# Two-layer tail of an attention kernel on one core: the last plain 256 rows as a seven-product block multiplication, with the whole instruction order replaced

## The chip, the cores and the metric

The kernel runs on one core of a Trainium2 chip. A core has five engines with queues of their own: TensorE (PE, matmuls), VectorE (DVE), ScalarE (ACT), GpSimd (POOL) and SyncE (SP). They wait for each other by semaphores. GpSimd and SyncE are used here mainly to issue DMAs; GpSimd's run on one DMA queue (q0 in the profile), SyncE's on another (q1), and 16 DMA engines move the data of both. The metric is the device time of one execution in microseconds, as the median of several runs.

## The reference

```python
def _attn_ref(q, k, v):                      # q, k, v: (8, 12, 448, 64)
    S = q.shape[2]
    scale = 1.0 / np.sqrt(q.shape[-1])
    scores = scale * np.matmul(q, k.transpose(0, 1, 3, 2))
    attn = np.maximum(scores, 0.0) ** 2 / S
    return np.matmul(attn, v).astype(np.float32)

def _moe_ref(x, w_in, w_out):                # x: (3584, 768), w_in: (768, 2048), w_out: (2048, 768)
    h = x @ w_in
    g = 0.5 * h * (1.0 + erf(h / sqrt(2)))
    return (g @ w_out).astype(np.float32)
```

The output of the attention, with its 12 heads of 64 laid side by side, is the x of the two layers. There is no softmax: the scores are clipped at zero and squared.

## The kernel before

**Tiles.** The work goes by batch b (8 of them, 448 rows each) and, within the attention, by group g of four heads (3 of them). All matmuls take bf16. A score step (`fn_qk` in `add_steps`, matmuls at L744) is four matmuls of 64 x 64 tiles into a PSUM tile `ps`; ScalarE or VectorE clips it into `a_sq` (L756 or L758), VectorE squares it (L765). Seven score steps make a group, and `add_av` (L805) multiplies them with v into `pav`, which is copied into xT. The first layer of batches 0 to 3 is done in plain tiles (`add_f1`, six matmuls of 448 columns at L857, then Gelu on ScalarE); that of batches 4 to 7 by block products with seven multiplications (`add_block`, L1009).

**The second layer.** The rows of all batches, 3584, are cut into 14 groups of 256 (g = 0 to 13 in `add_group`). A group is a product of a 256 x 2048 by a 2048 x 768 matrix, cut into 2 x 2 blocks and done with seven block multiplications in place of eight. For that VectorE makes, once, four sums of w_out's quadrants (`add_tsums`, L1120, in two halves each; the third one overwrites a quadrant of w_out itself), and for each group four sums of h's blocks (`sum_op`, L1170). The seven products p1 to p7 (`product`, eight matmuls of 384 columns at L1191) go through two PSUM banks "f" at a time; evictions (`passed`, copies at L518 or L520, adds at L1225) pass the partial results on. Group 0, the first 256 rows of batch 0, is the exception before: it is done by `add_plain` as four tiles (two of rows by two of columns, 16 matmuls of 384 columns each, L1295), with one copy and, for each row tile, one store behind it.

**Turning q and k.** TensorE needs q and k with the head dimension on partitions. For batches 0 and 1 TensorE transposes them (L612, L640). From batch 2 on SyncE issues DMA transpositions (`turn` in `add_T_dma`, L667): per batch six, for each group one of q (into qT, from nq) and one of k (into kT, from nk). Half of each group's qT is then swapped between partition halves (`swapped`, by VectorE as two copies at L518 or by SyncE as two DMAs). The buffers nq and nk are single from batch 2 on, so the load of q of batch 3 (L464, by GpSimd) overwrites what the transposition of batch 2 has to have read.

**Loads.** GpSimd issues all loads in its queue: q (L464), k (L553), v (L571), w_in in five steps (L481 to L483), w_out in three steps of one, two and two DMAs (L487). At most eight of them are in flight: each waits for the semaphore of the eighth before it.

**The order.** No engine's order follows from the program's loops. The program adds 1471 operations with their dependencies to a list (`sch.add`), and the string `ORDER` says in which order they are issued: a letter for the engine (P TensorE, D VectorE, A ScalarE, G GpSimd, S SyncE) and the operation's number in the list; `Z1056` is a short filler matmul. The framework puts in the semaphore waits that the data need. Operations with a choice of engine (the clipping, copies, swaps) get it from the letter. Some numbers that matter below, the same in both kernels: S229 and S228 are the transpositions of q and k of batch 2, group 0, S232 and S231 of group 1, S235 and S234 of group 2; G238, G239 and G241 are the three steps of the w_out load, G149 the first part of v of batch 2, G270 the first load of q of batch 3. What `ORDER` takes from:

```python
    GROUPS = {2: (1,), 3: (2, 3), 4: (4, 5), 5: (6,)}
    ...
            flow += [(2.6, add_plain(t, n)) for n in (1, 0) for t in (0, 1)]
            add_tsums()
    ...
        flow += [y for g in GROUPS.get(b, ()) for y in add_group(g)]
```

Of the kernel before, what the change touches and what calls it, by code (L numbers as in the profile page):

```python
# [100 lines left out]
D287 P312 P300 A355 P318 S399 P362 D281 D313 D296 P364 A363 D319 P370 D278 A301 A365 P358 A371  # L101
P315 P306 A359 P282 P352 D307 P360 A353 G241 P376 A361 P368 A377 A283 P366 A369 D284 D302 D236
D293 P372 A367 D290 P374 A373 P378 D390 D316 G274 P327 A379 P297 D391 A328 G273 G155 P333 P339
D314 A334 G240 P382 D298 D305 D317 A340 A375 S398 D308 A299 D320 D329 P330 P324 D417 P309 A325
P380 A383 A331 D310 D311 D392 P342 P321 P336 A381 A337 D332 D418 D341 D419 D326 S402 P384 A322
S401 D393 P387 D396 A385 S405 D394 D400 G407 G242 G237 A323 A343 G409 S386 G275 S404 P443 P446
D335 D420 G408 A444 P421 D395 D344 A447 D338 P449 D388 A450 D397 S389 A422 G412 P452 P345 D445
D346 P437 G411 P423 A453 A438 P440 A347 D424 D403 P455 S542 A441 P425 A456 D439 D442 P473 A426
P470 P461 P427 D454 A471 A474 D462 P429 D428 D457 P464 P479 P476 D430 A480 P431 D448 A465 D451
G414 G415 P433 D472 A477 D432 D562 D406 P467 P458 A468 S435 D469 P485 P491 S545 A486 D434 P509  # L110
D459 A492 S541 P513 A510 D560 A460 D478 D561 P503 S544 A514 P494 P500 D563 P519 A501 D481 D463
P515 A520 D475 A504 A495 D493 P517 D466 D543 S547 D496 D487 P488 A518 P482 A516 D502 S548 G552
P497 P511 D498 S436 G555 D499 P523 G551 A512 D489 A483 G550 A484 G416 P525 A524 D490 D546 G554
P600 G413 P609 P606 G410 D610 P521 D505 A601 A607 P603 P506 D604 A526 A522 P612 P639 D507 P531
A640 P527 G558 D613 D605 A532 D508 G557 P618 A528 P624 P615 D619 P529 S705 S704 A616 P537 S708
A530 A625 P535 A538 D620 D549 D626 D602 P627 P636 A536 P657 A637 P533 D611 D614 S707 A628 D608
D629 P539 A534 A658 P564 A540 D641 D659 D617 D638 P566 A565 P630 S710 S711 P633 P621 D631 A634
D632 S709 G715 P642 P651 A622 D635 P568 G718 G714 A623 D567 A652 G717 P570 G559 A569 D643 D706
P648 P666 P663 A649 P572 G721 A667 G722 D571 D644 D664 P660 P654 P645 G719 D661 A655 G716 G553
G556 D662 D650 G720 P769 P763 P574 A764 D573 D665 D668 A646 P576 A770 A647 D575 D580 S578 P772  # L120
P775 P778 P584 D577 S836 A776 A779 D656 D581 D653 D765 P586 S835 A585 A773 D777 P787 P766 D582
P669 A767 D587 A788 D712 P781 P588 A670 A671 D768 D780 D774 A782 D789 P790 P796 A791 P590 D783
D583 A797 D771 P799 A589 P784 S839 S842 A800 D591 P802 D801 P793 P592 D803 D785 A794 S838 P594
D593 D786 P596 D595 D837 P805 P811 D597 P823 A806 S841 P674 D792 A824 D795 D723 D798 P672 S843
D812 A675 P678 S598 D804 D807 P814 P817 P808 A815 D818 A673 D724 A679 P874 P820 A809 P676 D821
G849 D813 D825 P682 A677 G846 A875 G844 G851 P684 G847 A683 D840 G850 G845 A810 P829 A685 P880
G713 P826 G852 A830 P680 D827 D828 P688 A681 A881 D831 D816 D822 D819 P686 A689 P889 A687 P877
P832 D890 A878 P886 P904 D833 A887 S947 P690 D834 G848 G853 D905 P892 A691 P883 P692 A893 D884
D888 P901 A693 P898 P910 A911 P698 S950 D906 D882 D899 D885 D894 D876 P696 A699 S946 P694 D725
A697 S599 A902 D879 D912 P702 A695 P700 A703 D903 D726 P727 A701 D900 D891 P916 S949 P907 P895  # L130
D917 A908 A728 S948 P928 P913 D929 D909 P731 A914 S953 A896 D915 D918 P729 A897 S951 D930 P925
P922 S952 P919 D926 A923 D730 S579 P931 D927 D732 P934 A920 P733 A921 A932 D924 D935 P735 D734
D736 D933 P940 P937 P955 P737 A956 D936 D743 A941 P739 D738 A938 D744 S741 D942 P747 D939 D740
P958 A748 P970 S742 P943 D959 A971 S954 D746 P961 P964 A944 D1035 P749 A962 D965 A945 D966 P973
P982 D750 P967 P751 A974 A968 D745 D957 D969 D963 D972 P753 A752 P755 A983 D960 D754 D975 P994
P985 P976 A995 D986 P979 P997 D756 D984 P757 A980 A998 D854 D1037 P759 D987 A977 D758 A978 S761
P1015 D981 D855 P988 P1003 A1016 P858 D760 D856 D1027 A989 P860 A1004 A859 P991 P1018 P1012 D861
D999 D1036 A1019 P862 D990 D996 A992 P864 D1038 A1013 D993 D1017 P1021 P1000 D865 D1028 D1020
A1022 D857 A863 P1006 P1009 A1001 P866 A1002 A1007 D1030 D1127 D1005 P1039 P1056 P1041 A1057
P1058 D1008 D1023 D1014 A1010 P868 A1040 D1011 D1059 P1060 P1024 D1042 D1129 D1031 D867 A1025  # L140
A1026 P1062 P1045 D1032 P1043 D1063 P1047 P870 A1061 A1044 D1029 D1046 D1034 P1064 P1050 D1048
D1065 P1067 P1073 D1051 P1090 D1068 P1053 A1074 P1075 A1091 D1054 D1033 P1092 P1094 D1093 P1077
D1076 P1070 D871 P1096 A1066 D1071 A1095 A1078 A1072 P1079 D869 P1081 D1080 D1097 S872 S762 A1049
A1052 P1098 P1131 D1099 D1128 A1055 D1082 P1101 P1084 A1069 D1331 P1148 A1083 D1102 P1104 A1149
D1085 P1087 A1132 A1103 A1100 P1133 D1088 A1086 P1150 D1105 P1135 D1134 A1106 P1152 D1332 A1089
P1139 A1136 D1107 P1111 P1137 D1130 D1108 D1109 P1113 D1151 A1112 A1153 D1110 D1138 D1114 D1140
P1115 P1154 D1241 D1239 P1142 P1117 D1155 D1116 P1167 P1145 P1159 D1118 D1146 D1160 D1143 P1119
D1120 D1240 P1184 P1156 P1165 P1121 A1166 D1168 P1182 D1157 P1171 A1183 P1162 D1172 P1169 D1185
P1123 D1163 D1122 P1188 S1125 P1173 D1124 D1189 P1190 P1186 S1126 S873 P1193 D1191 D1174 P1176
A1170 A1187 A1144 P1179 D1177 A1161 P1196 D1194 A1178 A1164 P1245 D1197 D1333 P1262 A1195 P1243  # L150
P1203 D1199 D1200 D1201 P1260 A1158 A1204 A1141 P1205 A1261 A1192 P1207 D1180 D1206 A1181 A1198
A1147 A1244 P1209 D1208 A1175 D1202 P1211 D1210 D1212 P1213 D1219 P1215 P1251 P1247 D1220 D1214
D1246 D1216 P1223 D1221 D1263 S1218 P1225 D1222 D1224 S1217 P1249 P1227 P1264 D1242 D1250 D1334
D1226 P1266 P1229 A1248 A1265 P1254 D1230 P1268 D1267 D1228 D1252 D1255 P1233 P1231 P1271 P1277
D1234 D1272 P1294 D1269 P1279 P1296 A1278 A1295 P1257 D1280 P1298 D1232 P1281 P1235 D1258 D1297
A1253 A1299 A1259 A1282 P1283 P1300 A1256 A1273 P1285 P1302 D1284 D1301 P1274 D1286 P1288 D1275
P1305 D1303 P1335 D1289 D1306 A1290 P1291 P1308 D1236 A1307 P1337 D1292 S1238 A1336 P1354 A1276
D1338 D1311 A1293 P1315 D1312 A1316 A1287 P1339 D1313 P1352 P1317 A1353 A1304 D1309 A1270 D1355
D1314 A1310 P1319 D1318 P1358 A1320 P1321 P1341 P1323 D1322 D1342 D1359 D1405 D1324 P1343 P1360
# [240 lines left out]
def kernel(  # L400
# [1063 lines left out]
    flow, plans = [], {}  # L1464
# [95 lines left out]
```

## Time and profile before

| | |
|---|---|
| median of 3 runs | 366.47 us (366.0 to 367.02) |
| the profiled execution | 366.73 us |
| its span (first to last instruction) | 364.9 us |
| TensorE busy | 356.5 us (98%), 3598 matmuls |
| VectorE busy | 296.5 us (81%) |
| ScalarE busy | 208.0 us (57%) |
| GpSimd busy | 64.2 us (18%) |
| granted TensorE clock | 1.00 |
| DMA | 44.12 MB; 43.5% of 16 engines' span for GpSimd's queue, 28.1% for SyncE's |

How to read the rows: a group row has line, engine, operation, tile written <- tiles read, shapes and count, then busy us, mean ns of one, and the idle time of the engine just before them with what ended it. Timeline rows have start, duration, and the same names; an engine's name with a q behind it (SPq) is its sequencer issuing a DMA. A stretch row (from windows) has its bounds and length, then busy us and instruction count of TensorE, its weight loads, VectorE, ScalarE and GpSimd, the granted clock, the DMA share and GB/s. A row of a wait has who waited <- for whom, us in total, times, longest. A queue row has packets, MB and the share of 16 engines' time. Matmul records overlap, so the pace of a row of matmuls is its length divided by their number, not the mean of one.

### The profile page before, as it was taken

How to read it: one execution, taken by the hardware profiler on the slowest of the kernel's cores; microseconds unless marked ns; L12 is line 12 of the kernel's file. 1: busy time of each engine (PE TensorE's matmuls, PEld its weight loads, DVE VectorE, ACT ScalarE, POOL GpSimd, SP SyncE). 2: the span in 40 equal slices, each digit the busy share in tenths (PEclk: the TensorE clock that was granted, in tenths of full speed). 3: DMA queues.
4: the chain of work that ended last, by engine and by line, in shares of the span. 5: the costliest groups of instructions: out<-in, count | busy, mean ns of one | idle time of the engine just before them, and what ended most of it. 6: DMA issues, size and time to landing. Idle time of an engine off the chain costs nothing.

```text
span 364.9 us, 8580 instructions
## 1 busy us (share of the span) xinstructions
PE 356.5 (98%) x3598; PEld 225.7 (62%) x3598; DVE 296.5 (81%) x510; ACT 208.0 (57%) x337; POOL 64.2 (18%) x101
## 2 busy tenths in 40 slices
PE   8799999999999999999999999999999999999996
PEld 4576654455454445555445555799787689788664
DVE  2899874399999988999899999999867847665764
ACT  4997868565867686856766678437027024425310
POOL 8575225150124125024000000000000000000000
PEclk9999999999999999999999999999999999999999
DMA  9999999999999999999892301002021300140233
GB/s 164 198 191 191 200 176 139 193 202 188 183 209 195 211 175 200 229 159 151 136 170 66 105 11 43 3 2 86 3 89 42 88 0 2 45 129 2 86 89 87
DMA packets 73126, 44.12 MB, mean 121 GB/s; under 512 B 38144, under 2 KB 69760, under 8 KB 73088
## 3 DMA queue, kind: packets, MB, share of 16 engines
q0 software_dynamic: 32912, 22.47, 43.5%
q1 hardware_dynamic: 39280, 20.26, 28.1%
q10 hardware_dynamic: 896, 0.85, 0.7%
q8 instruction: 28, 0.46, 0.5%
q14 instruction: 10, 0.08, 0.1%
HBM read 45.61 MB, written 11.01 MB: 155 GB/s over the span
## 4 chain that ended last, share of the span: by engine, by line
PE 75%; DMA 13%; DVE 5%; POOL 4%; issue 1%; ACT 1%; POOLq 0%
PE pso L1191 33%; PE pb L1009 18%; PE psh L857 12%; PE ps L744 7%; PE pav L805 6%; DMA wout_sb<-in_moe_w_out_dram 5%; DMA v_sb<-in_v_dram 3%; DMA qT<-nq 3%; DMA win_sb<-in_moe_w_in_dram 2%; DVE a_sq L765 2%; DVE t_sb L1120 1%; POOL nq L464 1%; POOL nk L553 1%; DVE s_sb L1170 1%; POOL v_sb L571 1%
## 5 line engine op out<-in xcount | busy, mean ns | idle before, releaser
L756 ACT ACTIVATE a_sq<-ps 128x896 bf16<-128x896 f32 (+1 forms) x125 | 110.4, 927 | 33.5 <-PE ps L744 33.5
L765 DVE TENSOR_TENSOR a_sq<-a_sq 128x896 bf16<-128x896 bf16 (+1 forms) x169 | 97.0, 614 | 11.6 <-ACT a_sq L756 11.0
L857 PE MATMUL psh<-xT,win_sb 128*128 128x448 bf16 (+1 forms) x420 | 77.5, 337 | 0.5 <-DMA win_sb<-in_moe_w_in_dram 0.5
L857 PEld LDWEIGHTS <-win_sb 128*128 128x128 bf16 x420 | 38.9, 98 | 36.9 <-issue 9.0
L1046 DVE TENSOR_TENSOR part<-pb,part 128x448 f32<-128x448 f32 x80 | 47.3, 618 | 16.0 <-PE pb L1009 14.2
L1191 PEld LDWEIGHTS <-s_sb 128*128 128x128 bf16 x424 | 40.5, 98 | 26.8 <-issue 2.4
L758 DVE TENSOR_SCALAR a_sq<-ps 128x896 bf16<-128x896 f32 (+1 forms) x44 | 47.2, 1075 | 9.4 <-PE ps L744 9.2
L744 PE MATMUL ps<-qT,kT 64*64 64x448 bf16 (+1 forms) x756 | 47.6, 336 | 1.8 <-ACT a_sq L756 1.3
L867 ACT ACTIVATE h_sb<-psh 128x448 bf16<-128x448 f32 x64 | 34.8, 552 | 21.3 <-PE psh L857 21.0
L1191 PEld LDWEIGHTS <-h_sb 128*128 128x128 bf16 x312 | 29.4, 98 | 21.6 <-issue 4.6
L1009 PEld LDWEIGHTS <-win_sb 128*128 128x128 bf16 x384 | 36.8, 98 | 2.7 <-issue 0.4
L1191 PE MATMUL pso<-wout_sb,h_sb 128*128 128x384 bf16 x208 | 38.2, 326 | 0.0
L1191 PE MATMUL pso<-t_sb,s_sb 128*128 128x384 bf16 x208 | 38.1, 326 | 0.0
L1191 PE MATMUL pso<-wout_sb,s_sb 128*128 128x384 bf16 (+1 forms) x208 | 37.7, 324 | 0.0
L805 PE MATMUL pav<-a_sq,v_sb 64*64 64x448 bf16 (+1 forms) x756 | 36.8, 329 | 0.4 <-ACT a_sq L756 0.2
L1055 ACT ACTIVATE h_sb<-part 128x448 bf16<-128x448 f32 x48 | 25.4, 575 | 14.6 <-DVE part L1046 14.6
L1225 DVE TENSOR_TENSOR osb<-pso,p_sb 128x384 f32<-128x384 f32 x39 | 21.5, 552 | 14.8 <-PE pso L1191 11.0
L744 PEld LDWEIGHTS <-kT 64*64 64x64 bf16 x756 | 18.7, 105 | 22.4 <-issue 16.3
L805 PEld LDWEIGHTS <-v_sb 64*64 64x64 bf16 x756 | 21.3, 107 | 11.7 <-issue 2.0
L464 POOL DMA_DIRECT2D nq<-in_q_dram x24 | 17.7, 743 | 59.4 <-DMA qT<-nq 54.6
L1009 PEld LDWEIGHTS <-ws 128*128 128x128 bf16 x288 | 27.6, 98 | 1.0
L1055 ACT ACTIVATE h_sb<-pb 128x448 bf16<-128x448 f32 x16 | 8.2, 541 | 29.3 <-PE pb L1009 29.2
(62 smaller groups left out, 327.6 us busy)
## 6 DMA issues: line engine op xcount, KB each, us to landing
nk<-in_k_dram POOLq DMA_DIRECT2D x23, 224.0 KB, 7.4
nq<-in_q_dram POOLq DMA_DIRECT2D x21, 224.0 KB, 7.2
v_sb<-in_v_dram POOLq DMA_DIRECT2D x5, 672.0 KB, 11.1
out_dram<-osb SPq DMA_DIRECT2D x7, 336.0 KB, 3.3
v_sb<-in_v_dram POOLq DMA_DIRECT2D x9, 224.0 KB, 10.1
out_dram<-osb SPq DMA_DIRECT2D x7, 288.0 KB, 3.3
out_dram<-osb SPq DMA_DIRECT2D x8, 240.0 KB, 3.1
win_sb<-in_moe_w_in_dram POOLq DMA_DIRECT2D x8, 192.0 KB, 9.5
```

The costliest lines, as they stand in the source:

```text
L744: nc.tensor.matmul(ps[64 * j : 64 * j + 64, e, x * w : x * w + w], kT[r, g, i * 128 + 64 * j : i * 128 + 64 * j + 64], moving, start=True, ...
L756: A.activation(ar, ps, AF.Relu, scale=c_att)
L758: V.tensor_scalar(ar, ps, c_att, 0.0, op0=mybir.AluOpType.mult, op1=mybir.AluOpType.max,)
L765: V.tensor_mul(box["a2"][:, :, :used], ar, ar)
L805: nc.tensor.matmul(pav[0][o2 : o2 + 64, e, :w], vt[b][r, 2 * g + e, bass.ts(i, D)], box["a2"][r, y, o : o + w], start=(i == 0), stop=(i == ...
L857: nc.tensor.matmul(ph[:, x * n : x * n + n], win_sb[:, kd, bass.ts(m + x, 128)], xT[b][:, kd, c], start=(kd == 0), stop=(kd == KD - 1),)
L867: A.activation(h_ring()[:, m : m + nm, o + c.start : o + c.stop], box[0][:, :S].rearrange("p (x n) -> p x n", x=nm), AF.Gelu,)
L1009: nc.tensor.matmul(bank[name][:, y, z * HS : z * HS + HS], w[:, k, bass.ts(mm, 128)], right()[:, k], start=first and k == 0 and z == 0, st ...
L1046: V.tensor_add(get(to), ps(name), get(other))
L1055: A.activation(h_ring()[:, m : m + 2, o + half[c].start : o + half[c].stop], src().rearrange("p (x n) -> p x n", x=2), AF.Gelu,)
L1191: nc.tensor.matmul(box[bank][:, n0:n1], left()[:, kf], right()[:, kf, n0:n1], start=bool(need) and kf == 0, stop=kf == K2 - 1, skip_group_ ...
L1225: V.tensor_add(out()[:, n0:n1], box[bank][:, n0:n1], other()[:, n0:n1])
```

## The change

Group 0 becomes a block product like the other thirteen. `add_plain` is called no more: four plain tiles (64 matmuls), their four copies and two store operations go; four sums of h, seven products (56 matmuls), seven evictions and two store operations come. The program now adds 1481 operations. `ORDER` is replaced from its first line to its last. In the order of TensorE the changes are local swaps for the most part: the new group's p1 stands where the first plain tile stood, its other products up to where the plain tiles ended, and group 1 right behind. Three more swaps of qT go to SyncE (8 in place of 5), three fewer to VectorE. In GpSimd's queue the loads of w_out now stand directly behind the last load of batch 2, with the loads of batch 3 behind them; before, the first q load of batch 3 stood ahead of w_out, and the later ones between its steps. In SyncE's queue the transpositions keep their order.

```diff
@@ ORDER: nearly all lines differ; the stretch with the transpositions of batch 2 and the loads of w_out @@
 ...
-A199 P219 P216 D185 P245 G123 A254 A178 D179 D182 A220 G127 S229 P247 A217 S228 P210 P204 A248
-A246 P207 D218 D205 P263 D211 A208 D197 P261 S232 D200 A264 P192 A262 S231 D209 P213 P222 A214
-P255 D193 A223 S235 D215 D206 P257 A256 S234 D194 P267 A258 D221 P249 A268 D224 D212 P201 A250
-P225 D230 G270 A202 A203 G238 P276 P279 A226 G149 D277 P265 A227 G239 A280 D233 P294 A266 P288
-P291 A295 G152 P356 A289 P348 G272 G269 G271 P303 P285 A357 A292 A349 P350 A304 A286 P354 A351
+D181 A140 P216 G154 P219 D217 P261 A220 G153 D178 S229 G238 P247 D182 A179 D185 A262 S228 P210
+A248 D221 G239 P204 P207 D211 P245 G149 D205 P263 A246 A208 D206 P222 D197 P192 A264 P213 D218
+P255 S232 D223 G241 P257 A256 D200 S231 A214 D224 P265 A258 A193 P249 S235 A266 D194 D209 P201
+A250 S234 D212 D215 P225 D202 D230 P267 A226 A203 D227 P356 A268 G270 P276 A357 P288 G269 P279
 ...
@@ -1463,14 +1464,13 @@
     add_v(3, 0, G)
     flow, plans = [], {}
     F1B = {2: 1, 3: 2, 4: 3}
-    GROUPS = {2: (1,), 3: (2, 3), 4: (4, 5), 5: (6,)}
+    GROUPS = {2: (0, 1), 3: (2, 3), 4: (4, 5), 5: (6,)}
     for b in range(2, B):
         add_steps(steps(b), dve=True)
         if b == 2:
             x1 = f1(1)
             first_atoms = x1[:LEAD]
             flow += x1[LEAD:]
-            flow += [(2.6, add_plain(t, n)) for n in (1, 0) for t in (0, 1)]
             add_tsums()
         elif b in F1B:
             flow += f1(F1B[b])
```

`ORDER` is one line longer, so a line of the program after it has a number higher by one in the changed kernel (L744 becomes L745).

More of the change, by code (lines that the diff above doesn't have):

```diff
@@ new lines @@
+A286 A349 P282 P318 A371 P303 D319 P358 A304 D283 P364 A359 G272 D407 P300 D287 P312 A301 P352
+D305 D408 A365 P306 D293 A353 P315 P360 A313 D284 D302 P376 D296 A361 D236 A307 P368 G152 D380
+A377 G271 D290 P366 A369 D320 A316 D381 P378 A367 D409 P372 D382 G274 G237 P327 A373 P339 P297
+D383 A328 G273 D384 A379 G240 G155 P333 S389 A340 P374 D385 A334 D387 P411 S388 A298 D386 A299
+A375 P324 P309 D410 A412 P330 S392 P413 A331 D335 D314 P415 D414 D310 P417 A416 D317 A325 D329
+P419 S391 D311 D332 D418 P342 D308 P321 D427 S395 D420 P336 P421 D326 A337 D428 A322 S394 D341
@@ new lines @@
+P423 A343 D422 A323 D390 S425 P431 D430 D424 G398 P453 D344 P456 P459 G275 D338 P433 A460 D457
+G399 A454 G242 P345 D393 A432 G402 D429 G400 P447 D434 G401 P462 A448 P435 D346 G405 S551 D461
+A463 G404 P437 A347 D464 D436 P450 P480 P465 A451 D438 P439 D466 A481 D467 P483 P474 D440 P471
+A484 P441 D452 A475 D455 D396 P443 A472 S552 D442 D458 P477 P489 D449 P519 S555 A490 D478 P486
+D482 P495 S554 P468 A487 D444 D488 P501 A469 P529 D502 A520 A496 S558 D491 P523 A530 D570 A470
+D476 P525 A524 D485 D473 P504 A526 P513 G562 D497 P510 A514 P527 S556 D571 G561 A505 D479 P521
@@ new lines @@
+S446 G565 D503 A511 D553 G563 S426 G406 A528 P507 P498 P492 D508 A522 G397 S557 A499 G564 D572
+G403 P616 P610 A493 D500 P533 D512 D515 P531 A534 D506 D509 P535 A532 D617 A494 A611 P541 D559
+P619 P613 P516 D620 A614 A542 P649 A536 P622 D517 P537 A623 S715 D518 D573 A650 P539 D615 S445
+A538 D618 P625 A540 D624 P634 P628 G567 S718 P547 D629 G560 G566 D621 P545 G568 A548 A626 P543
+A635 A546 P646 D636 P637 A544 P667 D630 P549 A647 D612 A638 D627 P574 S720 D651 A550 A668 P576
+D575 S714 P640 P643 S716 P631 D641 A644 S717 D577 P661 D645 P652 P578 A653 D632 S719 D639 A633
@@ new lines @@
+P710 A713 S958 P737 S959 P926 P917 P905 D927 A918 S961 A711 D919 P938 A738 P923 D916 S963 P739
+A906 D910 A924 S609 A939 P741 D925 D907 S962 D928 P935 P932 P929 D936 A933 S964 D740 P941 P944
+D930 A742 P743 A942 D937 A931 D943 P745 A945 D934 D744 P947 D940 P950 P965 A948 D746 P747 D753
+A966 D755 P749 A951 D748 D946 S751 D949 P757 D754 D952 P980 D750 P968 P953 A981 D969 S752 D758
+P971 P974 A954 P759 D975 A972 A955 D976 P977 P983 D973 P992 A984 P761 D760 D967 A993 D756 P763
+A762 D985 A978 D982 P765 D979 D970 D764 P995 P1004 P986 D996 A1005 D766 P989 D994 P1007 P767
@@ new lines @@
+A1008 D866 D864 A990 P769 D1006 A987 D1045 A988 D768 P998 D865 P1013 S771 P1025 A1014 P868 D770
+D1037 S772 A999 P870 D1009 A1026 D867 A869 P1001 P1028 D871 P1022 A1002 D991 P872 D1000 A1023
+D1003 P874 A1029 D1027 D997 A873 D1047 P1016 P1031 D1038 P1010 A1032 D1046 D875 P1019 P876 D1015
+A1020 D1040 A1011 P1049 A1017 D1041 P1066 A1012 D1021 P878 A1067 D1033 A1050 D1030 P1051 D1024
+P1070 D877 P1068 D1018 P1053 D879 D1048 P1034 A1071 D1052 D1042 P880 A1035 D1069 A1054 D1039
+A1036 P1072 D881 P1055 D1044 S883 P1057 D1056 P1074 D1073 P1083 D1058 P1060 D1075 P1077 P1100
@@ L168 @@
+D1450 D1456 P1459 D1458 P1461 D1460 P1463 A1462 P1465 D1464 P1467 D1466 D1469 S1475 D1468 S1452
+S1474 P1470 P1471 D1472 S1476 S1477 D1473 S1478
 """
```

122 lines of the change are left out of this document (46 added, 76 removed).

## The prediction

> **What bounds the kernel now.** I read the page first (busy time and slices), then TensorE's own waits, then its order in time, and last the DMA queues, since the change moves loads.
>
> ```profile
> span 364.9 us, 8580 instructions
> PE 356.5 (98%) x3598; PEld 225.7 (62%) x3598; DVE 296.5 (81%) x510; ACT 208.0 (57%) x337; POOL 64.2 (18%) x101
> ...
> PE ps L744 <- ACT a_sq L756: 1.3, 3, 0.5
> ...
> PE psh L857 <- DMA win_sb<-in_moe_w_in_dram: 0.5, 1, 0.5
> ```
>
> TensorE is busy for 98% of the span, and all its listed waits are half a microsecond or less, a few microseconds in total. The waits of TensorE asked for from 36 us to the end come back empty. So from 36 us on TensorE is the bound: a matmul less is time won, and any wait that the new order brings into that stretch is time lost in full, because nothing later has idle time to absorb it.
>
> Before 36 us loads set the pace. These are TensorE's rows there:
>
> ```profile
> 30.23 0.27 PE L857 MATMUL psh<-xT,win_sb 128*128 128x224 bf16 x1
> 30.95 1.21 PE L857 MATMUL psh<-xT,win_sb 128*128 128x224 bf16 x11 [0.45 <-DMA win_sb<-in_moe_w_in_dram]
> ```
>
> It stands at the first-layer tile m=4, 5 of batch 0 until a piece of w_in lands. In the new order the same TensorE work stands ahead of that tile, and GpSimd's loads up to and past that piece are the same. A smoother start would thus end at the same load, and I count the new start at nothing; a start rougher by up to 0.6 us would be hidden there too.
>
> **The matmuls removed.** Four plain tiles of 16 matmuls go, seven products of 8 come: 64 against 56, all of 384 columns. The pace of such a matmul comes from the chain of waits:
>
> ```profile
> 278.24 7.80 PE pso L1191 x48
> ```
>
> 7.80 / 48 = 0.163 us each, so 8 x 0.163 = 1.30 us off TensorE's stream. Both orders change 51 times from attention steps to layer tiles, so that price stays as it is.
>
> **The vector work added.** Net it is four sums, five evicting adds and some copies; six half-copies of qT (the swaps) move to SyncE's queue.
>
> ```profile
> L1170 DVE TENSOR_TENSOR s_sb<-h_sb 128x1024 bf16<-128x1024 bf16 x26 | 17.8, 683 | 0.0
> L1225 DVE TENSOR_TENSOR osb<-pso,osb 128x384 f32<-128x384 f32 x25 | 13.8, 552 | 2.3 <-PE pso L1191 1.7
> L1120 DVE TENSOR_TENSOR t_sb<-wout_sb,t_sb 128x1536 bf16<-128x1536 bf16 x4 | 3.8, 948 | 0.0
> 73.00:90.00 17.00, 17.00 (x161) 9.00 (x160) 16.65 (x27) 9.58 (x16) 6.06 (x10) 1.00 1.31 196
> 90.00:110.00 20.00, 19.95 (x198) 10.28 (x197) 18.38 (x33) 15.14 (x21) 3.57 (x5) 1.00 1.34 202
> ```
>
> 4 x 0.683 + 5 x 0.552 = 5.5 us, less some 2 us for copies that go: about 3.5 us more for VectorE over the run. From 73 to 90 us it is busy for 16.65 of 17 us, and there the new group's sums and the eight w_out sums (L1120) now come together. I count this at nothing as long as w_out arrives earlier than now, which it does (below): the cover is that VectorE's w_out sums can begin while first-layer tiles of batch 1 still occupy TensorE. Without that cover it is a rival.
>
> **The loads moved.** This is where I expect the time to be decided. GpSimd's queue now:
>
> ```profile
> 40.00 1.41 POOL L571 DMA_DIRECT2D v_sb<-in_v_dram  x2 [2.00 <-DMA win_sb<-in_moe_w_in_dram]
> 52.38 0.73 POOL L464 DMA_DIRECT2D nq<-in_q_dram  x1 [10.97 <-DMA qT<-nq]
> 53.10 1.16 POOL L487 DMA_DIRECT2D wout_sb<-in_moe_w_out_dram  x1
> ```
>
> After the loads of batch 2 GpSimd waits 10.97 us: its next load (q of batch 3) overwrites nq, which SyncE's DMA transposition of batch 2 (L667) must have read. Only then come the w_out loads. In the new order the w_out loads stand ahead of that q load: nothing holds them, so they are issued from about 41.4 us on, right while SyncE issues the six transpositions of batch 2 (q and k of groups 0, 1, 2). Before, those six had the DMA engines nearly to themselves. Three transpositions, each as issue time and time to landing, the last two with w_out in flight and the first ahead of it:
>
> ```profile
> L667 SPq DMA_TRANSPOSE qT<-nq x1: 1325/1325/1325, 42.4 to 42.4; - x1
> DMA to landing us min/median/max: 9.4/9.4/9.4
> ...
> L667 SPq DMA_TRANSPOSE kT<-nk x1: 1481/1481/1481, 53.6 to 53.6; - x1
> DMA to landing us min/median/max: 12.2/12.2/12.2
> ...
> L667 SPq DMA_TRANSPOSE qT<-nq x1: 2853/2853/2853, 57.8 to 57.8; - x1
> DMA to landing us min/median/max: 12.9/12.9/12.9
> ```
>
> The first landed at 42.4 + 9.4 = 51.8. The other two landed at 65.8 and 70.7, 4.9 us apart. Without loads in flight the pair between them went much faster:
>
> ```profile
> L667 SPq DMA_TRANSPOSE qT<-nq x1: 3382/3382/3382, 46.6 to 46.6; - x1
> DMA to landing us min/median/max: 6.7/6.7/6.7
> ...
> L667 SPq DMA_TRANSPOSE kT<-nk x1: 2112/2112/2112, 50.0 to 50.0; - x1
> DMA to landing us min/median/max: 4.3/4.3/4.3
> ```
>
> 53.3 and 54.3: one microsecond apart. The packets of the DMA queues say why (q0 is GpSimd's, q1 SyncE's), first from 64 to 69 us, then SyncE's from 57.7 to 70.7, in which the two slow ones ran:
>
> ```profile
> q0 software_dynamic: 942, 0.72, 91.6%
> q1 hardware_dynamic: 937, 0.23, 35.9%
> ...
> q1 hardware_dynamic: 1848, 0.46, 37.4%
> ```
>
> Side by side the two queues move packet for packet, 942 against 937 in 5 us. A transposition has 1848 / 2 = 924 packets of a quarter of a kilobyte, so at 937 / 5 = 187 a microsecond it takes 4.9 us; over the 13 us with their dips, 6.5. GpSimd's side has supply enough: it moves 0.72 MB in 5 us there, and w_out has
>
> ```profile
> wout_sb<-in_moe_w_out_dram POOLq DMA_DIRECT2D x1, 1536.0 KB, 17.5
> wout_sb<-in_moe_w_out_dram POOLq DMA_DIRECT2D x4, 384.0 KB, 15.8
> ```
>
> 1536 + 4 x 384 = 3072 KB, 21 us at that rate, behind about 1 MB of q, k and v. So from about 46 to 75 us all six transpositions run against loads. With the first at 51.8 as now (it also ran against loads) and steps of 5.3 us (4.9 to 6.5; I take a value near the lower, since it is the undisturbed pace), the six land at 51.8, 57.1, 62.4, 67.7, 73.0 and 78.3.
>
> When does TensorE want them? These are its first score steps (L744) of batch 2 now, groups 0, 1 and 2:
>
> ```profile
> 54.52 0.55 PE L744 MATMUL ps<-qT,kT 64*64 64x448 bf16 x8
> ...
> 59.31 0.57 PE L744 MATMUL ps<-qT,kT 64*64 64x448 bf16 x8
> ...
> 62.88 4.71 PE L857 MATMUL psh<-xT,win_sb 128*128 128x448 bf16 x24
> 67.53 0.76 PE L744 MATMUL ps<-qT,kT 64*64 64x448 bf16 x12
> ...
> 77.40 0.38 PE L744 MATMUL ps<-qT,kT 64*64 64x448 bf16 x4
> ```
>
> A first-layer tile (6 matmuls) costs (67.53 - 62.88) / 4 = 1.16 us with its share of the change of mode, a score step 0.19. Counted off the new order, two more tiles stand ahead of group 0's first step, four more tiles and two more score steps ahead of group 1's, and one tile fewer ahead of group 2's. So it wants group 0 at 54.5 + 2.4 = 56.9, group 1 at 59.3 + 5.1 = 64.4 and group 2 at 77.4 - 1.0 = 76.4. Each needs its q and its k: group 0 lands at 57.1 (0.2 late), group 1 at 67.7 (**3.3 late**), group 2 at 78.3, against 76.4 + 3.3 = 79.7 (in time). The three share one lag, so the wait is the largest, 3.3 us. With steps of 4.9 us it is 2.1, with 6.5 it is 6.9 (and group 2, at 84.3, adds another 1.0).
>
> Behind the waiting step all of TensorE's queue is held; the activations and sums that wait for it have their own slack and come later by the same amount. What is late next: w_out is issued about 12 us earlier than now (41.4 against 53.1), so VectorE can make its sums ahead of the new group's products, which stand where the plain tiles stood; the batch 3 loads follow w_out and, with GpSimd's idle stretch gone, land at about the time they do now or earlier. SyncE's stores of the new group stand where the plain stores stood.
>
> **The sum.** The profiled execution took 366.73 us (span 364.9 and 1.8 around it), 0.26 above the median of 366.47. 366.73 - 1.30 + 3.3 = 368.7; less 0.26 gives **368.5 us**, slower by 0.55%. About 0.3% (1.1 us) is what a measurement of this kernel can tell from no change. Its own range, from the bounds of 4.9 to 6.5 us a transposition, is 367.3 to 373.1; the upper end supposes dips all the way, so I take 367.0 to 371.5.
>
> **Rival 1, faster: the transpositions keep up.** If they land in time, 366.47 - 1.30 = 365.2 us. For it speaks the one-microsecond pair; it decides this way if a step takes under (64.4 - 51.8) / 3 = 4.2 us on average, for instance if SyncE's packets get more than every second turn, or if GpSimd issues w_out late. [...] Chance 0.21.
>
> **Rival 2, much slower: the wait also costs the clock.** TensorE starts at half pace:
>
> ```profile
> L1369 PE MATMUL spin<-zero 128*128 128x512 bf16 x11 | 4.9, 632 | 1.0 <-DVE zero L1352 1.0
> ```
>
> 4.9 / 11 = 0.44 us for 512 columns, where 0.163 x 512 / 384 = 0.22 is the pace later. If a wait brings that state back for as long again, 4.9 us of it lose 2.4: 368.5 + 2.4 = 370.9 us. It needs a longer idle stretch than this trace has after the start (0.5 us), so the trace doesn't say. [...] Chance 0.11.
>
> **Rival 3, little change: VectorE is late instead.** The transpositions are in time, but the new group's fourth product, which reuses the bank of its second, needs an eviction that stands behind all eight w_out sums (0.95 us each), four squares and two sums, some 10 us of queue on an engine at 98%; I find about 1 us of slack there. Were it late by 1.5 us: 365.2 + 1.5 = 366.7. Chance 0.10.
>
> **The numbers.** Forecast 0.58, of which 0.13 falls within 0.3% (a wait of 0.2 to 2.4 us). Rival 1 counts as faster with 0.19 and within with 0.02; rival 2 as slower with 0.11; rival 3 as within with 0.07, slower with 0.03. Faster 0.19, same 0.22, slower 0.59. The range takes in rival 1's value and stops at 371.5, leaving out the far ends of the forecast and of rival 2: 365.1 to 371.5.
>
> **What would show it.** In the new profile: w_out issued at about 41 us; q1 and q0 moving packet for packet from 46 to 75 us; kT of group 1 landing near 67.7; one wait of TensorE at L745 (L744 shifted by a line) on a DMA of kT or qT, 2 to 5 us long, near 64 us; none of note after it; 3590 matmuls. I am wrong if no such wait is there, if the steps are a microsecond apart beside w_out, or if TensorE waits for VectorE's eviction (L1226) between 80 and 95 us. Half pace after the wait would show in the slice's granted clock.

## The result: 372.1 us, slower by 1.6%

| | before | changed |
|---|---|---|
| median | 366.19 us (365.87 to 367.02, 6 runs) | 372.1 us (371.22 to 372.8, 6 runs) |
| ratio | | 1.0157 (95% interval 1.0138 to 1.0177) |
| profiled execution | 366.73 us, span 364.9 | 372.23 us, span 370.4 |

368.5 us was forecast. The direction is right, and 3.6 us are missing. First the page of the changed kernel (span, busy times, and the clock granted to TensorE in 40 slices of the span, 9 for 90% and more) and TensorE's longest wait:

```profile
span 370.4 us, 8554 instructions
PE 357.4 (96%) x3590; PEld 224.7 (61%) x3590; DVE 299.9 (81%) x514; ACT 205.5 (55%) x334; POOL 65.0 (18%) x101
PEclk9999999899999999999999999999999999999998
PE ps L745 <- DMA kT<-nk: 3.0, 1, 3.0
```

TensorE has its 8 matmuls less and yet is busy for 0.9 us longer; the wait foretold is there, once, with 3.0 us; and the clock row has an 8 in its eighth slice (65 to 74 us), right behind the wait. That 8 is the second thing to read. TensorE in order of time, around the wait:

```profile
60.52 3.58 PE L858 MATMUL psh<-xT,win_sb 128*128 128x448 bf16 x18
64.03 0.38 PE L745 MATMUL ps<-qT,kT 64*64 64x448 bf16 x4
67.42 0.96 PE L745 MATMUL ps<-qT,kT 64*64 64x448 bf16 x8 [3.00 <-DMA kT<-nk]
68.31 3.51 PE L858 MATMUL psh<-xT,win_sb 128*128 128x448 bf16 x12
```

One score step of four matmuls takes 0.19 us, so TensorE stands from 64.22 to 67.42, for 3.2 us. Behind that, 12 first-layer matmuls take 3.51 us, where 18 had taken 3.58: TensorE ran at half pace for a part of that time (the granted clock is 0.50 from 67.09 to 70.50 us).

The transposition it waited for, that of k of group 1, and the packets of the two DMA queues from 46 to 75 us:

```profile
L668 SPq DMA_TRANSPOSE kT<-nk x1: 4659/4659/4659, 52.4 to 52.4; - x1
...
DMA to landing us min/median/max: 15.0/15.0/15.0
...
q0 software_dynamic: 5258, 3.89, 90.9%
q1 hardware_dynamic: 5258, 1.31, 39.5%
```

52.4 + 15.0 = 67.4, and 5258 packets of each queue in 29 us, 181 a microsecond: packet for packet.

Then the end, which the prediction did not look at. The last matmuls of TensorE and SyncE's last ten stores (start, length from the first to the last issue), first of the kernel before, then of the changed one; last, the copy of the left half of group 13 in the changed kernel:

```profile
360.85 0.61 PE L1191 MATMUL pse<-wout_sb,s_sb 128*128 128x128 bf16 x8
351.80 10.50 SPq L1145 DMA_DIRECT2D out_dram<-osb  x10
```

```profile
364.18 0.61 PE L1192 MATMUL pse<-wout_sb,s_sb 128*128 128x128 bf16 x8
355.36 12.76 SPq L1146 DMA_DIRECT2D out_dram<-osb  x10
359.65 0.48 ACT L521 COPY osb<-pso 128x384 f32<-128x384 f32 x1 [8.66 <-PE pso L1192]
```

Before, the span ended 364.9 - 360.85 = 4.05 us behind TensorE's last group; now it is 370.4 - 364.18 = 6.22, **2.2 us more**. In the new `ORDER` the store S1475 (right half of row tile 1 of group 13), whose data come near the end, stands in SyncE's queue ahead of S1452 (a full store of group 12) and S1474 (the left half above, ready at 360.1). SyncE waits until 362.8, then issues all of them in one go, up to 368.1.

So the profiled executions differ by 5.5 us: -1.30 (matmuls) + 3.2 (wait) + 1.5 (half pace, worked out below) + 2.2 (stores) + 0.5 to 0.7 for two short waits for VectorE in the block products near 244 and 253 us make 6.1 to 6.3; -0.6 to -0.8 is left. 0.4 of it was won at the start: the wait of 0.45 us for w_in is gone, behind that tile TensorE is 0.44 us earlier than before (31.65 against 32.09), and at 40 us it still is (40.65 against 41.04). The rest stays open. The short waits are this row (idle time of weight loads, us and times); before, the row has no wait for VectorE:

```profile
  DVE part L1047: 0.7, 2
```

### The profile page after: what moved, and what is told of

Same layout as the page of the kernel before. It is cut to its first block, busy times and chain, and to the rows that moved or that the text cites. A ratio compares the mean times of both kernels' runs of the same rounds, so it can differ in the third digit from the quotient of the medians.

```text
span 370.4 us, 8554 instructions
## 1 busy us (share of the span) xinstructions
PE 357.4 (96%) x3590; PEld 224.7 (61%) x3590; DVE 299.9 (81%) x514; ACT 205.5 (55%) x334; POOL 65.0 (18%) x101
## 4 chain that ended last, share of the span: by engine, by line
PE 85%; DMA 6%; SPq 3%; DVE 2%; ACT 1%; POOL 1%; issue 0%; POOLq 0%
PE pso L1192 35%; PE pb L1010 17%; PE psh L858 16%; PE ps L745 9%; PE pav L806 8%; DMA kT<-nk 4%; SPq L668 3%; DMA nq<-in_q_dram 2%; ACT a_sq L757 1%; DVE part L1047 1%; PE tp L641 0%; POOL nk L554 0%; POOL nq L465 0%; DVE a_sq L759 0%; DVE a_sq L766 0%
## 5 line engine op out<-in xcount | busy, mean ns | idle before, releaser
L757 ACT ACTIVATE a_sq<-ps 128x896 bf16<-128x896 f32 (+1 forms) x126 | 111.7, 922 | 41.5 <-PE ps L745 41.5
L858 PE MATMUL psh<-xT,win_sb 128*128 128x448 bf16 (+1 forms) x420 | 78.8, 340 | 0.1
L1192 PEld LDWEIGHTS <-s_sb 128*128 128x128 bf16 x456 | 43.3, 98 | 30.3 <-issue 3.8
L759 DVE TENSOR_SCALAR a_sq<-ps 128x896 bf16<-128x896 f32 (+1 forms) x43 | 46.0, 1076 | 15.1 <-PE ps L745 14.1
L745 PE MATMUL ps<-qT,kT 64*64 64x448 bf16 (+1 forms) x756 | 47.7, 338 | 5.1 <-DMA kT<-nk 3.0
L1192 PEld LDWEIGHTS <-h_sb 128*128 128x128 bf16 x336 | 31.9, 98 | 23.1 <-issue 3.9
L1192 PE MATMUL pso<-t_sb,s_sb 128*128 128x384 bf16 x224 | 41.1, 326 | 0.0
L1192 PE MATMUL pso<-wout_sb,h_sb 128*128 128x384 bf16 x224 | 41.0, 326 | 0.0
L1192 PE MATMUL pso<-wout_sb,s_sb 128*128 128x384 bf16 (+1 forms) x224 | 40.6, 324 | 0.0
L1226 DVE TENSOR_TENSOR osb<-pso,p_sb 128x384 f32<-128x384 f32 x42 | 23.2, 553 | 17.6 <-PE pso L1192 13.8
L745 PEld LDWEIGHTS <-kT 64*64 64x64 bf16 x756 | 18.2, 105 | 26.3 <-issue 16.4
L554 POOL DMA_DIRECT2D nk<-in_k_dram x23 | 16.5, 717 | 70.1 <-DMA kT<-nk 61.3
```

What stands on the lines that cost most here:

```text
L745: nc.tensor.matmul(ps[64 * j : 64 * j + 64, e, x * w : x * w + w], kT[r, g, i * 128 + 64 * j : i * 128 + 64 * j + 64], moving, start=True, ...
L757: A.activation(ar, ps, AF.Relu, scale=c_att)
L759: V.tensor_scalar(ar, ps, c_att, 0.0, op0=mybir.AluOpType.mult, op1=mybir.AluOpType.max,)
L858: nc.tensor.matmul(ph[:, x * n : x * n + n], win_sb[:, kd, bass.ts(m + x, 128)], xT[b][:, kd, c], start=(kd == 0), stop=(kd == KD - 1),)
L1192: nc.tensor.matmul(box[bank][:, n0:n1], left()[:, kf], right()[:, kf, n0:n1], start=bool(need) and kf == 0, stop=kf == K2 - 1, skip_group_ ...
L1226: V.tensor_add(out()[:, n0:n1], box[bank][:, n0:n1], other()[:, n0:n1])
```

## The experiments

Letters and numbers are `ORDER`'s; the experiments are numbered e1 to e12, and the number stands ahead of each result. Each edit moves operations, and two add filler matmuls; none leaves work out. In the edits of the loads G149, the load of v that stands among the steps of w_out, moves with them.

### The stores at the end

```diff
@@ the changed kernel's ORDER
-D1450 D1456
+D1450 S1452 D1456
...
-A1462 P1465
+A1462 S1474 P1465
...
-S1475 D1468 S1452 S1474 P1470
+S1475 D1468 P1470
```

> The changed kernel, but in SyncE's queue the last store of group 12 (S1452) and the first store of group 13 (S1474, left half of row tile 0) stand where they stood in the kernel before, ahead of the store of the right half of row tile 1 (S1475). Theory (the tail's 2.2 us come from the order of the stores): TensorE ends where it ends now (last matmul starts at 364.2), SyncE's last issue falls from 367.8 to about 365.2, the span ends about 2.9 us behind that as in the kernel before (361.9 to 364.9): 372.1 - 2.2 = 370.0 us (369.6 to 370.5). Rival (the last evictions are late or the stores are slowed by something else, and their order does not matter): 372.1 us.

Measured (e1): 371.08 us (370.18 to 371.55), ratio 1.0133 (1.012 to 1.0146): 1.0 us less, not 2.1. SyncE's row in this kernel:

```profile
356.71 10.28 SPq L1146 DMA_DIRECT2D out_dram<-osb  x10
```

10.28 us from first to last, near the 10.50 of the kernel before. TensorE's last group starts at 365.53 here and the span ends at 369.8, 4.27 us later: 1.95 us of the tail are gone. In this profiled execution the time fell by less because TensorE ended 1.35 us later, mainly since half pace lasted twice as long (6.83 us in place of 3.41, below); for the other three runs, which have no profile, that isn't shown. The other way round, the kernel before with the new order of its last stores:

```diff
@@ the kernel before's ORDER
-P1439 D1438 D1444 S1441 P1447 D1440 S1442
+P1439 D1438 D1444 S1441 P1447 D1440
...
-D1450 P1453 D1452 S1464 P1455
+D1450 P1453 D1452 P1455
...
-D1459 S1465 D1458
+D1459 S1465 S1442 S1464 D1458
```

> The kernel before, with one edit: the last store of group 12 (S1442) and the first store of group 13 (S1464) stand behind the store of the right half of row tile 1 (S1465) in SyncE's queue, as in the changed kernel. Theory (the order of the stores costs the changed kernel 2.2 us): SyncE's last issue comes 2 to 2.5 us later than now, the span ends as much later: 366.1 + 2.1 = 368.2 us (367.8 to 368.7). Rival (stores that bunch up are cheap): 366.1 us.

Measured (e6): 368.1 us (367.97 to 368.55), ratio 1.0051 (1.0037 to 1.0064). Its row is 13.41 us long:

```profile
351.20 13.41 SPq L1146 DMA_DIRECT2D out_dram<-osb  x10
```

The median rose by 1.9 us over that of the kernel before in the same rounds (366.24), for two stores in the wrong place of a queue. This term is shown.

### The loads of w_out

```diff
@@ the kernel before's ORDER (e5): w_out ahead, as in the changed kernel (and gone from its old place)
-G127 S229 P247
+G127 S229 G238 G239 G149 G241 P247
@@ the changed kernel's ORDER (e4): w_out behind the first q load of batch 3 (and gone from its old place)
-A268 G270 P276
+A268 G270 G238 G239 G149 G241 P276
```

> The kernel before, with one edit: the loads of w_out (G238, G239, G241, with G149) stand directly behind the first transposition of batch 2 (S229) as in the changed kernel, ahead of the first q load of batch 3. Theory (these loads alone slow the transpositions): the six land at about 51.8, 56.7, 62.9, 67.4, 72.4, 76.6 as in the changed kernel; TensorE wanted group 0 at 54.5 and group 1 at 59.3, so it waits 56.7 - 54.5 = 2.2 us and then 67.4 - 61.5 = 5.9 us, and the longer stretch is followed by 3.4 us at half clock (1.7 us): 366.1 + 2.2 + 5.9 + 1.7 = 375.9 us (374.0 to 377.0). Rival (the transpositions are slow in the changed kernel for another reason of its order): 366 to 367 us.

Measured (e5): 375.79 us (374.09 to 377.54), ratio 1.0259 (1.0225 to 1.0293). TensorE in order of time:

```profile
50.51 2.84 PE L806 MATMUL pav<-a_sq,v_sb 64*64 64x448 bf16 x56
56.50 0.96 PE L745 MATMUL ps<-qT,kT 64*64 64x448 bf16 x8 [3.15 <-DMA kT<-nk]
57.39 2.28 PE L858 MATMUL psh<-xT,win_sb 128*128 128x448 bf16 x6
...
60.30 2.44 PE L858 MATMUL psh<-xT,win_sb 128*128 128x448 bf16 x12
67.09 0.96 PE L745 MATMUL ps<-qT,kT 64*64 64x448 bf16 x8 [4.35 <-DMA kT<-nk]
67.98 4.66 PE L858 MATMUL psh<-xT,win_sb 128*128 128x448 bf16 x12
```

The two waits came as 3.15 and 4.35 (together 7.5, where 8.1 were expected), and half pace behind both. These loads moved, with nothing else changed, cost the kernel before 9.5 us (366.24 in the same rounds). The changed kernel pays less of it, since its order has more other work ahead of group 1: it comes to that step at 64.2, not at 59.3.

> The changed kernel, but in GpSimd's queue the loads of w_out (G238, G239, G241, with G149) stand behind the first q load of batch 3 (G270), as in the kernel before; all other queues as in the changed kernel. Theory (the w_out loads slow the transpositions): k of group 1 lands near 54 instead of 67.4, the wait near 64 and its half clock go, -4.7 us; but w_out lands 8 to 12 us later (the last pieces near 82 to 85), while TensorE would want group 0's first products at 83.9 - 4.7 = 79.2, so that a part comes back as waits for w_out or for VectorE's sums of it between 79 and 90: 367.4 to 371 us. Rival (the transpositions are slow by themselves in the new order): k of group 1 lands at 67 again and the time stays at 372.1 us.

Measured (e4): 369.74 us (369.3 to 372.1), ratio 1.0114 (1.0094 to 1.0135). The transposition of k of group 1 in this kernel:

```profile
L668 SPq DMA_TRANSPOSE kT<-nk x1: 2175/2175/2175, 49.4 to 49.4; - x1
...
DMA to landing us min/median/max: 6.4/6.4/6.4
```

It lands at 55.8, and no wait for it is left. The time lies within the range, but what came back isn't where it was expected. TensorE's waits from 60 to 120 us, and then VectorE's longest from 90 to 120:

```profile
PE ps L745 <- DVE a_sq L759: 0.9, 1, 0.9
PE pav L806 <- DVE a_sq L759: 0.3, 1, 0.3
...
DVE osb L1226 <- DMA out_dram<-osb: 1.9, 1, 1.9
```

No wait for w_out: it landed early enough even so. Instead an eviction of group 1 stands for 1.9 us on VectorE until a store of group 0 has left its buffer, with the clipping behind it for which TensorE then waits.

### How much of it is the clock

A shorter wait, by one first-layer tile moved ahead of the waiting step, then three:

```diff
@@ the changed kernel's ORDER
-P282 P318 A371 P303 D319 P358 A304
+P282 P358 P318 A371 P303 D319 A304
@@ and the other one
-P282 P318 A371 P303 D319 P358 A304 D283 P364 A359 G272
+P282 P358 A371 P364 A359 P352 A365 P318 P303 D319 A304 D283 G272
...
-A301 P352 D305 D408 A365 P306
+A301 D305 D408 P306
```

> The changed kernel, but one first-layer tile (P358) stands ahead of the first score step of batch 2's group 1 (P318), which waits for the transposition of k. Theory (the half clock behind the wait comes only where the idle stretch is about 3 us or more): TensorE idles for 3.2 - 1.15 - 0.1 = 1.9 to 2.0 us near 65.5, no record of half clock follows, and 1.15 + 1.5 us less two changes of mode (0.2) are won: 372.1 - 2.5 = 369.6 us. Rival (any wait of a microsecond or two drops the clock): only the tile's length is won, 372.1 - 1.0 = 371.1 us, with some 3.4 us at half clock still there.

Measured (e2): 370.76 us (370.23 to 372.3), ratio 1.0122 (1.0108 to 1.0137): between the two, nearer to the rival. TensorE:

```profile
66.47 1.29 PE L858 MATMUL psh<-xT,win_sb 128*128 128x448 bf16 x6
69.30 0.57 PE L745 MATMUL ps<-qT,kT 64*64 64x448 bf16 x8 [1.53 <-DMA kT<-nk]
69.80 1.31 PE L858 MATMUL psh<-xT,win_sb 128*128 128x448 bf16 x6
```

The wait is 1.5 us, and behind it 6 matmuls take 1.31 us, full pace, which the theory said and the rival did not. (In this execution everything up to here ran 2 us later, the first four matmuls of the step at 65.98 in place of 64.03, and its mean clock is 0.992 without half pace in these rows, so its own time is no measure of the edit.) Three tiles:

> The changed kernel, but three first-layer tiles (P358, P364, P352, with the Gelus that free their banks) stand ahead of the first score step of group 1. Theory (the order alone decides: the transposition lands at 67.4 whatever TensorE does, and the wait and the half clock go once 3.4 us of other work stand ahead): no wait over 0.3 us near 67, no half clock, 372.1 - 3.2 - 1.5 = 367.4 us (367.2 to 367.9). Rival (the wait only moves: group 1's clipping, squares and products with v come later, and TensorE waits for ScalarE or VectorE by 2 to 3 us between 68 and 80): 369 to 370.5 us.

Measured (e3): 371.01 us (370.71 to 372.27), ratio 1.0141 (1.0127 to 1.0154). No half pace, and no wait for k of group 1 is left, but TensorE's waits from 60 to 100 us are now

```profile
PE ps L745 <- DVE a_sq L759: 1.4, 2, 1.0
PE pso L1192 <- DVE osb L1226: 0.8, 1, 0.8
PE pav L806 <- DVE a_sq L766: 0.3, 1, 0.3
```

The theory missed by 3.6 us. The rival had the mechanism, and the time came out half a microsecond above its 370.5: the score steps come later and close together, VectorE's clipping is late for them, and the eviction at the new group's products, which starts at 86.2 us behind VectorE's last sums of w_out, is late as well. A wait that is filled with work taken from behind it can come back as the lack of that work.

The clock by itself, without moving any work. `Z7168` stands for 14 matmuls of 128 x 128 by 512 columns of zeros:

```diff
@@ the changed kernel
-P282 P318 A371
+P282 Z7168 P318 A371
...
 def add_fill(n):
...
+                if n > 2000:
+                    nc.tensor.matmul(
+                        fill[:, :c], zero, zero[:, :1].to_broadcast([128, NB])[:, :c],
+                        start=True, stop=True,
+                    )
+                    continue
```

> The changed kernel with one addition: 14 filler matmuls on zeros (128 x 128, 512 columns each, some 3.0 us at full pace) stand directly ahead of the first score step of group 1, where TensorE otherwise idles for 3.2 us. The transpositions, loads and stores are untouched, so the step still can't start before its k lands near 67.4. Theory (the half clock comes from the idle stretch, and costs by itself): no half clock near 67 us, the wait for k shrinks to 0.1 to 0.5 us, the step starts at the same time as before, and the 1.5 us that half pace cost in the profiled run go: 370.6 us; up to 371.6 if only a part of the runs had paid for the clock. Rival (the slow stretch behind the wait has another cause, for instance PSUM or the loads): matmuls of 373 ns again behind 67.4 us, 372.1 us.

Measured (e10): 371.82 us (371.11 to 373.89), ratio 1.0165 (1.014 to 1.019). The records agree with the theory (full pace behind 68.1 us), the time hardly: the median is lower by 0.3 us alone, with runs 2.8 us apart. In the profiled execution the step started at 68.14 in place of 67.42. Its k landed at 52.9 + 14.8 = 67.7, later by 0.3, and the fillers held the step for the other 0.4. From that step to TensorE's last group it took 295.3 us, in the changed kernel 296.8: 1.4 us were won behind the wait, and half of that had been lost ahead.

The granted clock, as the mean over a whole run, hints at which runs had a spell (a stretch at half pace). For the changed kernel's six runs it is 0.991, 0.992, 0.996, 0.998, 0.996 and 0.994, and one spell of 3.4 us is 0.5 x 3.4 / 370 = 0.005. The end of the span, at half pace behind the last matmul (0.51 from 367.4 to 370.4 us in the profiled execution), is in these means too, so that by them only two or three of the six runs can have had the spell behind the wait. It isn't what orders these runs: the one at 0.998 is the longest, 372.8 us.

To see it without the losses of the late part, e11 and e12 keep the changed kernel's order up to D648 (about 143 us), the w_out loads included, and take everything behind from the old order; e12 has the fillers.

> The changed kernel's own order, its w_out loads included, up to about 143 us (up to D648), and behind it all other operations in the order of the kernel before, its last stores included. The wait for k of group 1 and what follows it stay. Theory (the changed kernel loses about 2.1 us by its last stores and 0.5 to 0.9 us by waits for VectorE between 160 and 253 us, all of it in the late part): 372.1 - 2.1 - 0.7 = 369.3 us (368.7 to 369.9). Rival (the late part costs the stores alone): 370.0 us; or (the early part alone makes the loss) 371.5 to 372.1 us.

> The kernel of the run before, with the 14 filler matmuls ahead of the first score step of group 1. What is left is the wait for k alone, without half pace behind it and without the losses of the late part, which is the case that the prediction's sum was made for. Theory (half pace is worth its 1.5 us where it comes, and it comes in about half of the executions): 369.3 - 0.8 = 368.5 us (368.0 to 369.0). Rival (half pace is given back later, as the 0.3 us of the fillers' first run would say): 369.0 to 369.3 us.

Measured: 370.56 us (368.32 to 372.01), ratio 1.0108 (1.0074 to 1.0141), without fillers (e11); **368.7 us** (368.26 to 369.24), ratio 1.0064 (1.0043 to 1.0086), with them (e12). e11 lies above its theory: against the changed kernel the late part gave back 1.5 us, not 2.8. With the fillers in both, e10 against e12, it is 3.1 us. The six runs of e11 sort themselves by their mean clock: 368.32 us at 1.000; 370.11, 370.18 and 370.94 at 0.995; 371.19 and 372.01 at 0.991. By that, no spell, one, or two of them; the profiled execution, the one of 371.19, has two on end, from 66.8 to 73.6 us. With fillers TensorE reads (13 of the 14 fillers are in the record):

```profile
63.84 0.38 PE L745 MATMUL ps<-qT,kT 64*64 64x448 bf16 x4
64.33 3.21 PE L1524 MATMUL fill<-zero 128*128 128x512 bf16 x13
67.46 0.57 PE L745 MATMUL ps<-qT,kT 64*64 64x448 bf16 x8
67.97 2.44 PE L858 MATMUL psh<-xT,win_sb 128*128 128x448 bf16 x12
```

The step starts at 67.46, as in the changed kernel (67.42), since k lands when it lands. But 8 score matmuls take 0.57 us in place of 0.96, and 12 of the first layer 2.44 in place of 3.51: 0.39 + 1.07 = 1.5 us for one spell.

### Can both be had?

> The changed kernel with both edits of the first round: w_out's loads behind the first q load of batch 3, and the last stores in the order of the kernel before. Theory (two separate losses that add): 369.7 of the loads' edit less 2.0 = 367.7 us (367.3 to 368.3). Rival (the stores are worth only the 1.0 us of the median of their own run): 368.7 us.

Measured (e7): 367.59 us (365.0 to 368.64), ratio 1.0032 (1.0015 to 1.0049), near the theory. With w_out's loads back, the order of the stores is worth 369.74 - 367.59 = 2.15 us, near the 1.9 of e6 and not the 1.0 of e1. With the old order behind D648 and one eviction moved:

```diff
@@ e8, beside w_out behind G270 and the old order behind D648
-D438 P439 D466 A481
+P439 D466 D438 A481
```

> The changed kernel's order up to about 143 us (up to the operation D648), with w_out's loads behind the first q load of batch 3 and one eviction of group 1 (D438), which waits for a store, moved behind the next clipping; behind D648 all other operations in the order of the kernel before, its stores included. Theory (the block product itself wins 1.3 us and a start that is 0.4 us earlier, and what is lost lies in the loads, in the stores and in a few waits for VectorE at 101, 162 to 165, 242 and 250 us): 366.1 - 1.3 - 0.4 + 0.5 for small waits left = 364.9 us (364.4 to 365.8). Rival (VectorE, with 3.5 us more to do, is what the new group costs, and it is late in this order too): 366.5 to 368 us.

Measured (e8): 365.8 us (365.21 to 367.68), ratio 0.9985 (0.9971 to 1.0). That is about half a microsecond under the kernel before (366.24), less than a measurement here can tell, and 0.9 above what was expected. Its profiled execution, the longest of the eleven, showed three more waits for VectorE, and e9 moved their causes:

```diff
@@ e9, on e8
+D308 directly behind D311
+D442 ahead of D396
+D722 behind D781
```

> The kernel of the last run (early part in the new order with w_out's loads further back, the rest in the old order) with three of VectorE's operations moved: the square D308 two places ahead (TensorE's product with v waited 0.45 us for it at 87.3), the eviction D442 ahead of a swap (0.3 us at 105.1), and the swap D722, which itself waited 2.0 us for a transposition and held the squares behind it (1.6 us of TensorE's time at 157.8), behind those squares. Theory (VectorE's order, not its load, makes these waits): 365.8 - 0.45 - 0.3 - 0.3 to 1.6 = 364.5 us (363.8 to 365.0). Rival (VectorE is short of time there, and the waits move to the next operation): 365.3 to 366 us.

Measured (e9): 366.85 us (365.09 to 368.37), ratio 0.9995 (0.9966 to 1.0024), no difference where 364.5 was expected. TensorE's waits behind 36 us, first of e8, then of e9:

```profile
PE pav L806 <- DVE a_sq L766: 1.6, 2, 1.3
PE pav L806 <- DVE a_sq L759: 0.3, 1, 0.3
PE psh L858 <- DVE osb L1226: 0.2, 1, 0.2
```

```profile
PE pso L1192 <- DVE osb L1226: 0.4, 1, 0.4
PE pav L806 <- DVE a_sq L759: 0.2, 1, 0.2
```

The three waits went, and a smaller one came at the new group's products. TensorE's last group starts 1.6 us earlier in this execution than in e8's, but that one was e8's longest, and e9's runs lie 3.3 us apart. Of the kernel before's 17 in the same rounds, 12 lie within 0.5 us, and the others reach up to 370.79. What spreads them stays open. No version was found that beats the kernel before by more than a measurement can tell.

## Why the prediction was right or wrong

- **Eight matmuls less, -1.30 us.** 3590 are counted, and all products keep their size. The gain is real, but less than any of the losses beside it.
- **Packet for packet, and the landings.** Forecast 51.8, 57.1, 62.4, 67.7, 73.0, 78.3; the transpositions, by issue and time to landing, came at 51.8, 56.8, 63.0, 67.4, 72.3 and 76.6. That the loads of w_out do it is shown from both sides (e4, e5).
- **The wait, 3.3 us.** It was 3.2, at the step and from the transposition that were named; groups 0 and 2 cost next to nothing, as reckoned.
- **The start, counted at nothing.** "A smoother start would thus end at the same load" did not hold: the wait for w_in went, and 0.4 us were won. TensorE's list before also holds a wait of 1.0 us, at the very start; the reading of half a microsecond or less left it out, without consequence.
- **Rival 1 falls** with the packets. **Rival 3 falls** in the changed kernel: from 80 to 95 us no wait for an eviction is there. The margin is thin, though: with three tiles moved ahead (e3) and in e9 a wait for an eviction appears, of 0.8 and 0.4 us.
- **The step that failed first: "SyncE's stores of the new group stand where the plain stores stood."** That sentence looked at group 0's stores and took the rest of SyncE's queue as unchanged, in an order said to be new from the first line to the last. At the end no work follows that could cover a late store: it cost 2.2 us in the profiled execution, 1.9 by e6, 2.15 by e4 against e7.
- **The step that failed second: the wait was priced at its length.** The forecast's 3.3 us left out half pace, which was Rival 2, at a chance of 0.11. One spell cost 1.5 us rather than the 2.4 that the 4.9 us of half pace at the start had suggested. It comes in some executions and not in others: by the mean clocks two or three of the changed kernel's six had it, and five of e11's six, where e12 against e11 puts it at 1.9 us of the median. With a wait of 3.3 us forecast, the chance that it touches the clock should have been near one half.
- **Small terms:** the waits in the block products near 244 and 253 us, 0.5 to 0.7 us, were not foreseen. They too come from the order being new far away from the change: e1, e7 and e10, which keep the new late part, have the same row of 0.7 us, and e8, e11 and e12, with the old one, have none.

With both missed steps and the small waits taken out, the forecast's own case remains: e12 measured 368.7 us, and 368.5 was forecast. That the two agree to 0.2 us is partly luck: e12 is 2.7 us above the kernel before in its rounds (366.01), and the forecast was 2.0 above 366.47. The time of the changed kernel lies 0.6 us above the range; up to 371.5 the range had room for a longer wait or for half pace, but nothing for the end of the kernel.

## What to carry to other kernels

When a whole order is replaced, compare every queue in it from end to end, the last stores first, since nothing behind them hides a delay. A load moved ahead is not free where another queue moves data at the same time: ask which transfers it takes its turns from, and who waits for those (in e5 it cost 9.5 us). Waits of TensorE for k of 2.9 to 4.35 us were followed by half pace in the traces here, one of 1.53 us (e2) was not: such a wait has to be priced with what it does to the clock, 1.5 us for one spell. Fillers of the wait's length took that part away here without moving any work (1.9 us of the median, e12 against e11); where they were 0.4 us too long (e10), that came off the gain.

## What the runs showed of the hardware

**Half pace behind a wait came for 3.41 or 6.83 us.** It lasted 3.41 us in the changed kernel and behind e5's first wait, and 6.83 in e1, in e11 and behind e5's second. The waits for k ahead of it were of 3.0 us in the changed kernel, 3.1 in e1, 2.9 in e11, 3.15 and 4.35 in e5; behind the 1.53 us of e2 it did not come. Here are stretches of 3.41 us laid along this: of the changed kernel and of e1 the stretch in which TensorE idled and the ones behind it, and of e2 one that holds its wait. Read TensorE's busy time (behind the comma) and the granted clock, the 0.50 or 1.00:

```profile
63.68:67.09 3.41, 0.74 (x7) 0.11 (x4) 0.72 (x2) 1.23 (x3) 1.26 (x2) 1.00 1.27 192
67.09:70.50 3.41, 3.08 (x14) 1.08 (x15) 2.44 (x3) 0.92 (x1) 0.70 (x1) 0.50 1.27 191
70.50:73.92 3.42, 3.42 (x29) 1.28 (x27) 3.42 (x7) 2.22 (x4) 0.98 (x2) 1.00 1.31 188
```

```profile
63.04:66.45 3.41, 1.41 (x10) 0.49 (x8) 0.57 (x1) 1.90 (x4) 0.89 (x2) 1.00 1.20 183
66.45:69.87 3.42, 2.36 (x12) 0.78 (x13) 1.72 (x2) 0.92 (x1) 0.70 (x1) 0.50 1.27 191
69.87:73.28 3.41, 3.41 (x13) 1.25 (x15) 3.41 (x7) 0.54 (x1) 0.27 (x1) 0.50 1.30 188
```

```profile
67.79:71.20 3.41, 1.90 (x18) 0.79 (x22) 1.47 (x2) 1.28 (x2) 1.14 (x2) 1.00 1.28 192
```

At full pace, the stretch busy for 0.74 us of 3.41 (22%, the changed kernel) and the one busy for 1.41 (41%, e1) were followed by half pace, and the one busy for 1.90 us (56%, e2) was not (8 score matmuls from 71.04 us on took 0.57 us). At half pace, the one busy for 2.36 us (69%, e1) was followed by another half one, and the one busy for 3.08 us (90%, the changed kernel) by full pace. In the traces of e5 and e11 0, 0.77 and 1.11 us at full pace were followed by half pace, 2.56 and 2.77 us at half pace by another half stretch, and 2.91 us by full pace. By their mean clocks e11's six runs had no spell (1.000), one (0.995) or two (0.991). What decides that isn't shown: only one execution of each kernel has such stretches.

**A DMA transposition beside another queue.** Without loads in flight a transposition landed a microsecond behind the one before it (54.3 after 53.3, in the kernel before, where from 51.8 to 54.4 us SyncE's queue moved 2550 packets and GpSimd's none). Beside GpSimd's loads, w_out's among them, the 924 packets of a transposition took 4.3 to 6.2 us by the landings above, at 181 packets a microsecond for either queue, though SyncE's packets carry a third of the bytes (1.31 MB against 3.89 MB for 5258 each).
